# Top-k attention and two gated layers on one core: softmax in place over three score buffers, batch factor on ScalarE, two transposed buffers, two accumulators

## The chip, the cores and the metric

The kernel runs on one core of a Trainium2 chip. Its time is the device time of one execution in microseconds. Beside the plain runs there is one profiled execution, and every row shown below comes from it.

## The reference

Attention over 4 batches, 8 heads, 576 positions of 64 dimensions, in which only the 32 largest scores of a row stay; then a layer 512 to 2048 to 512 with an ELU between, then a gated layer whose two arms are multiplied before a product with two more matrices.

```python
scores = scale * q @ k.T
kth = 32nd largest of each row
scores = where(scores >= kth, scores, -1e9)
attn = exp(scores - max); attn = attn / (sum(attn) + 1e-9)
x = (attn @ v) as [2304 tokens, 512]
h = x @ w_in;  g = where(h > 0, h, exp(min(h, 0)) - 1);  x = g @ w_out
out = ((x @ w1) * (x @ w2)) @ w3 @ w_out2
```

All inputs are float32. The kernel splits a float32 into a high and a low float16 part and multiplies high by high, high by low and low by high, so each product of the layers is three matmuls.

## The kernel before, in words

**Tiling.** 2304 tokens are nine chunks of two tiles of 128 tokens. For each chunk `attention` (L344) goes over four pairs of heads and two tiles, so there are 72 tiles of 128 tokens by 2 heads by 576 keys. `mlp` (L654) then runs the layers of the chunk over its 256 tokens, in units: A (first product and ELU), O (second product), Y (evacuation of the sum and a bound on its norm, from which a scale follows), B (the gated arms), D (last product and output). A chunk's units run one chunk after its attention.

**One attention tile.** TensorE makes the scores of half the keys in `psS` (L383) and ScalarE copies them to a score buffer `s` (L385), twice. VectorE finds the 32 largest of each row and head in place of a sort: four MAX8 (L392) and three MATCH_REPLACE8 (L394) for each head, on a work buffer `wk`. ScalarE computes the masked exponential with a PReLU of huge slope and an Exp (L407, L409) from `s` into a buffer `y`; ScalarE copies `y` to its high half in `pi` (L415), GpSimd subtracts to get the low half (L416), both over the two heads at once. Two transposing DMAs (L419), one for each head, bring `pi` to `pt`. TensorE multiplies `pt` by the values (L431) into the accumulator `psA`; column 64 of each head holds the sum of the weights. VectorE adds 1e-9 to the sums (L440), takes the reciprocal (L441), multiplies the rows of an older batch by the factor `phi` (L443), and multiplies the result by the reciprocal (L444). ScalarE and GpSimd split it (L447, L448), and a DMA transposes it into `x` (L449).

**Buffers.** Two score buffers `s`, two `y`, one `pi`, one `pt`, one `psA`. `psA` and `psN` (256 columns for the norm bound of unit Y, L729 to L735) are columns of one PSUM tile of 512 float32.

**Weights.** The weights come as 64-bit words. Each block is rebuilt to float32 (`load64`, L461: ScalarE, VectorE L477, GpSimd L479), its norm bounded, and scaled and split (`convert`, L499). This runs beside the first chunk's attention. `prep_v` gives each batch of values its scale `sv` and the ratio `phi` to the batch before; `scales` (L543) computes its reciprocal `rho` and constants of the layers.

**What sets the order.** Nothing runs when it is written. Each piece of work is recorded with `op(engine, cost, fn, reads, writes, priority)`. `Program.emit` (L79) plays the costs through a list scheduler: it has one queue for each engine, a latency for each pair of engines (L26), and takes among the ready ops of an engine the one with the lowest rank, where

```python
rank = [o[4] - PAR["cpw"] * cp[i] for i, o in enumerate(self.ops)]
```

The first term is the priority that the op was given, a multiple of STEP plus offsets from `PAR` (L33); the second is its longest path of costs to the end. The order it arrives at is the order in which each engine's instructions are written, and on the chip each engine then runs them in that order and waits where its inputs are late. Semaphores are put in by the tile framework from the tiles that instructions read and write, not from the names used in `op`.

Of the kernel before, what the change touches and what calls it, by code (L numbers as in the profile page):

```python
# [31 lines left out]

PAR = dict(whole=(), cd={'wi': [0, 0], 'wo': [0, 0], 'w34': [8, 0], 'w12': [16, 0]}, pv=115.601, pi=85.231, p34=-12.914, po=349.342, p12=114.078,   # L33
           pis=556.026, pos=-260.711, p12s=-169.557, p34s=-55.646, ci=133.963, co=-112.786, cos=-460.256, c12=-826.201, m34=-813.244, c34=-203.986, 
           m34s=2.143, h34=2, oq=90.567, os=18.83, ok=209.036, ot=363.395, orr=1387.061, opp=-709.446, oa=-95.859, ost=828.567, a0=104.812, a1=106.795, 
           lag0=49.33, lag=24.052, ho=2, h12=0, h12c=7, nr34=2, gm0=1, gm1=1, gm=1, bm=4, cpw=15.144, step=6600.0, pvb=-185.914)

# [112 lines left out]
def kernel(ctx: ExitStack, tc: tile.TileContext, qd, kd, vd, vn, w_in, w_out, w1, w2, w3t, w4, out,  # L150
# [54 lines left out]
    M8 = ring("m8", 4, [128, 2, 32], F32)  # L205
    TY = ring("ty", 4, [128, 16], F32)
# [137 lines left out]
    def attention(c, t0, n):  # L344
# [4 lines left out]
        for pair in range(4):  # L349
# [8 lines left out]
            for t in range(n):  # L358
# [15 lines left out]
                for half in range(2):  # L374
                    cols = slice(half * 288, half * 288 + 288)
                    pqk = pr + (PAR["os"] + .25 * half) * STEP
                    for kk, c0, c1 in ks:

                        def qk(qs=qs, kk=kk, t=t, cols=cols):
                            for i, (L, e) in enumerate(((QH, 0), (QH, 1), (QL, 0))):  # L380
                                for hh in range(2):
                                    hs = slice(64 * hh, 64 * hh + 64)
                                    T.matmul(psS[:, hh, 0:288], lhsT=L[qs][hs, t * 128:t * 128 + 128], rhs=KT[kk][hs, e, cols], start=i == 0, stop=i == 2)  # L383
                        op("PE", 420, qk, [("qh", qs), ("ql", qs), ("k", kk)], ["psS"], pqk)
                        op("ACT", 540, lambda sS=sS, cols=cols, c0=c0, c1=c1: A.activation(sS[c0:c1, :, cols], psS[c0:c1, :, 0:288], AF.Copy, scale=0.125), ["psS"], [sk], pqk)  # L385
# [12 lines left out]
                mx = m8[:, :, 0:1].rearrange("p a b -> p (a b)")  # L398
                tm, dn, ri = [ty[:, 2 * i:2 * i + 2] for i in range(3)]
# [11 lines left out]
                ps, pt = nxt("pi", NPI), nxt("pt", NPT)  # L411
                PIs, pk = PI[ps], ("pi", ps)
                p4 = pr + STEP * PAR["opp"]
                yks = [(*yk, 0), (*yk, 1)]
                op("ACT", 1053, lambda Y=Y, PIs=PIs: A.activation(PIs[:, :, 0:S], Y, AF.Copy), yks, [pk], p4)  # L415
                op("POOL", 2336, lambda Y=Y, PIs=PIs: G.tensor_tensor(PIs[:, :, S:2 * S], Y, PIs[:, :, 0:S], op=OP.subtract),  # L416
                   yks, [pk], p4 + .034 * STEP)
                for hh in range(2):
                    op("SP", 1050, lambda PIs=PIs, pt=pt, hh=hh: Q.dma_start_transpose(out=PT[pt][:, hh], in_=PIs[:, hh]), [pk], [("pt", pt, hh)], p4 - 1e6, lat=1406.0)  # L419
# [3 lines left out]
                p5 = pr + PAR["oa"] * STEP  # L423
                for bb, c0, c1 in segs:
                    vs = Vc[bb, pair]

                    def av(vs=vs, c0=c0, c1=c1, pt=pt):
# [4 lines left out]
                    op("PE", 850, av, [("v", vs), ("vl", vs), ("pt", pt, 0), ("pt", pt, 1)], ["psA"], p5)  # L432

# [4 lines left out]

                def xfin(xf=xf, dn=dn, ri=ri, r1=r1, vb=vb):
# [4 lines left out]
                    V.tensor_tensor(xf.rearrange("p (h d) -> p h d", h=2), psA[:, :, 0:64],  # L444
                                    ri.rearrange("p (h d) -> p h d", d=1).to_broadcast([128, 2, 64]), op=OP.mult)
                op("DVE", 360, xfin, ["psA", *([("phi", vb)] if r1 else [])], [("xf", fs), K("ri")], p5)
                op("ACT", 200, lambda xt=xt, xf=xf: A.activation(xt[:, 0:128], xf, AF.Copy), [("xf", fs)], [("xt", us)], p5)  # L447
# [70 lines left out]
    def prep_v(b, pr):  # L518

        P.tag = "w_v"  # L520
        pieces = []
        for i in range(4):
            if b == 0:
                dst, keys = W12T[:, 2 * i:2 * i + 2].rearrange("p a b -> p (a b)")[:, 0:S], [("w12", 2 * i), ("w12", 2 * i + 1)]
            else:
                rs = nxt("raw", 2)
                dst, keys = raw[rs][:, 0:S], [("raw", rs)]
            dma(dst, vn[b, :, i * S:i * S + S], 128 * S * 4, [], keys, pr)
            pieces.append((dst, keys, S))
        nv, sv, kb = scal(f"nv{b}"), scal(f"sv{b}"), ("nv", b)  # L530
        norm(pieces, nv, kb, pr)
        if b:
            tiny(lambda: V.tensor_tensor(nv, nv, scal(f"nv{b - 1}"), op=OP.max), [("nv", b - 1)], [kb], pr)
        d = sv.bitcast(I32)
        tiny(vts(d, nv.bitcast(I32), 1, 0x3F800000, OP.logical_shift_right, OP.bitwise_and), [kb], [("sv", b)], pr)
        tiny(vts(d, d, -1.0, float((189 + 15) << 23), OP.mult, OP.add), [], [("sv", b)], pr)
        if b:

            r, phi = tmp(16), scal(f"phi{b}")
            tiny(lambda: V.reciprocal(r, scal(f"sv{b - 1}")), [("sv", b - 1)], ["t16"], pr)  # L540
            tiny(lambda: V.tensor_tensor(phi, sv, r, op=OP.mult), [("sv", b), "t16"], [("phi", b)], pr)

    def scales(b, pr):  # L543

        P.tag = "w_v"
        r, phi = scal(f"rho{b}"), scal(f"phi{b}")
        tiny(lambda: V.reciprocal(r, phi), [("phi", b)], [("rho", b)], pr)
        tiny(lambda: V.tensor_tensor(scal(f"c1n{b}"), scal(f"c1n{b - 1}"), r, op=OP.mult), [("rho", b), ("c1n", b - 1)], [("c1n", b)], pr)
# [105 lines left out]
    def mlp(c, t0, n, dprev, pr0, span, hooks=None):  # L654
# [59 lines left out]
        def y_evac(pr):  # L714
# [10 lines left out]
            def gram():  # L725
                for t in range(n):
                    for k in range(4):
                        c = X[:, 0, k, t * 128:t * 128 + 128]
                        T.matmul(psN[:, t * 128:t * 128 + 128], lhsT=c, rhs=c, start=t == 0 and k == 0, stop=k == 3, skip_group_check=True)  # L729
# [3 lines left out]
            op("DVE", 80 + n * 135, lambda: V.tensor_reduce(n1, psN[:, 0:N], axis=AX.X, op=OP.max), ["psN"], [("n1", xs)], pr)  # L733
            op("PE", 240, lambda: T.matmul(psN[:, 0:128], lhsT=n1.to_broadcast([128, 128]), rhs=ident, start=True, stop=True), [("n1", xs), "ident"], ["psN"], pr)
            op("DVE", 200, lambda: V.tensor_reduce(n2, psN[:, 0:128], axis=AX.X, op=OP.max), ["psN"], [("n2", xs)], pr)  # L735
            tiny(vts(n2, n2, 1.02, 1e-30, OP.mult, OP.max), [], [("n2", xs)], pr)
# [174 lines left out]
```

## Time and profile before

| what | value |
|---|---|
| median of 3 runs | 1100.72 us (1099.6 to 1103.41) |
| the profiled execution's own time | 1098.79 us |
| its span | 1097.0 us |
| granted TensorE clock, mean | 0.976 |
| PE, DVE, ACT, POOL busy | 91%, 85%, 74%, 59% of the span |
| PE busy in 40 slices | `4199847699898999999999999999999999999998` |
| DVE busy in 40 slices | `6999899999999989999997999997999999971010` |

Engines: PE is TensorE's matmuls (PEld its weight loads), DVE VectorE, ACT ScalarE, POOL GpSimd, SP the queue of the DMAs. A slice is 27.4 us and a digit is the busy share in tenths. The busy share of PE is of matmuls that overlap, so it tells of back-to-back issue, not of a peak.

### The profile page before, as it was taken

The page shows a single profiled execution, that of the slowest core. Times are in us where ns is not written, and L with a number is a line of the kernel's source. Part 1 is how long each engine was busy: PE and PEld are TensorE (multiplying, and loading weights), DVE is VectorE, ACT ScalarE, POOL GpSimd, SP SyncE. Part 2 cuts the span into 40 slices and gives each one's busy share as a digit, 9 for nine tenths or more (in the row PEclk, how much of TensorE's full clock was granted, in tenths as well). Part 3 has the DMA queues.
Part 4 walks back from the last instruction along what each step waited for, and adds up shares of the span by engine and source line. Part 5 has one row for each costly group of instructions (what it writes and reads, how often), then busy time and mean ns, then how long its engine had stood idle before and what let it go on. Part 6 is the DMA issues. An engine that isn't in the chain of part 4 may idle for free.

```text
span 1097.0 us, 24651 instructions
## 1 busy us (share of the span) xinstructions
PE 996.1 (91%) x9452; PEld 759.1 (69%) x9452; DVE 935.9 (85%) x2024; ACT 807.7 (74%) x1349; POOL 652.0 (59%) x619
## 2 busy tenths in 40 slices
PE   4199847699898999999999999999999999999998
PEld 2144413368777868887886888788778878879875
DVE  6999899999999989999997999997999999971010
ACT  6976789899778966786795688689768857963522
POOL 5479765558536844783685478368537745853711
PEclk9999968799999999999999999999999999999999
DMA  9989973744736586456859545656664652231000
GB/s 364 319 234 339 290 239 129 197 115 109 149 88 177 172 187 147 103 125 163 178 170 224 141 103 113 173 144 166 165 162 97 134 138 71 50 82 37 1 20 20
DMA packets 238678, 165.54 MB, mean 151 GB/s; under 512 B 195808, under 2 KB 208608, under 8 KB 238560
## 3 DMA queue, kind: packets, MB, share of 16 engines
q1 hardware_dynamic: 238560, 163.97, 55.8%
q8 instruction: 74, 1.21, 0.5%
q14 instruction: 44, 0.36, 0.1%
HBM read 95.13 MB, written 21.61 MB: 106 GB/s over the span
## 4 chain that ended last, share of the span: by engine, by line
PE 57%; DVE 23%; ACT 6%; DMA 6%; issue 4%; POOL 3%; SPq 1%; DVEq 0%; POOLq 0%; ACTq 0%
DVE m L392 8%; DVE wk L394 7%; PE psS L383 5%; PE psR L672 4%; PE psR L751 4%; PE psA L431 4%; PE psR L674 4%; PE psR L673 4%; PE psY L709 4%; PE psR L753 4%; PE psR L752 4%; PE psY L710 4%; PE psY L711 4%; DMA pt<-pi 4%; DVE w L477 3%
## 5 line engine op out<-in xcount | busy, mean ns | idle before, releaser
L392 DVE MAX8 m<-wk 128x8 f32<-128x576 f32 x432 | 308.2, 746 | 0.0
L416 POOL TENSOR_TENSOR pi<-y,pi 128x1152 f16<-128x1152 f32 x72 | 172.8, 2400 | 118.5 <-ACT pi L415 108.1
L394 DVE MATCH_REPLACE8 wk<-m,wk 128x576 f32<-128x576 f32 x288 | 211.9, 741 | 0.0
L751 PE MATMUL psR<-x,w 128*128 128x256 f16 x576 | 157.8, 274 | 1.4 <-ACT t L761 1.4
L672 PE MATMUL psR<-x,win 128*128 128x256 f16 x576 | 157.7, 274 | 1.2 <-DMA x<-xt 1.2
L753 PE MATMUL psR<-x,w 128*128 128x256 f16 x576 | 157.4, 273 | 0.0
L752 PE MATMUL psR<-x,w 128*128 128x256 f16 x576 | 157.4, 273 | 0.0
L709 PE MATMUL psY<-g,wout 128*128 128x256 f16 x576 | 157.4, 273 | 0.0
L674 PE MATMUL psR<-x,win 128*128 128x256 f16 x576 | 157.3, 273 | 0.0
L673 PE MATMUL psR<-x,win 128*128 128x256 f16 x576 | 157.3, 273 | 0.0
L710 PE MATMUL psY<-g,wout 128*128 128x256 f16 x576 | 157.0, 273 | 0.3 <-POOL g L696 0.3
L711 PE MATMUL psY<-g,wout 128*128 128x256 f16 x576 | 157.0, 273 | 0.0
L407 ACT ACTIVATE y<-s,m 128x576 f32<-128x576 f32 x144 | 106.4, 772 | 51.1 <-DVE m L392 46.6
L383 PE MATMUL psS<-kt,qh 64*128 64x288 f32 x640 | 91.1, 362 | 35.3 <-ACT s L385 27.1
L385 ACT ACTIVATE s<-psS 128x576 f32<-128x576 f32 (+1 forms) x160 | 103.3, 646 | 20.8 <-PE psS L383 19.6
L409 ACT ACTIVATE y<-y,ty 128x576 f32<-128x576 f32 x144 | 108.6, 774 | 6.8 <-POOL ty L402 6.7
L392 DVE MAX8 m<-s 128x8 f32<-128x576 f32 x144 | 101.9, 744 | 7.6 <-ACT s L385 7.6
L394 DVE MATCH_REPLACE8 wk<-m,s 128x576 f32<-128x576 f32 x144 | 105.9, 741 | 0.0
L383 PEld LDWEIGHTS psS<-kt,qh 64*128 64x128 f32 x640 | 50.9, 195 | 70.8 <-ACT s L385 36.2
L696 POOL TENSOR_TENSOR g<-t,g 128x512 f16<-128x512 f32 x72 | 84.4, 1174 | 22.2 <-ACT g L695 21.7
L431 PEld LDWEIGHTS <-pt 128*128 128x128 f16 (+1 forms) x2240 | 80.5, 103 | 22.0 <-DMA pt<-pi 12.5
L431 PE MATMUL psA<-vv,pt 128*128 128x65 f16 (+3 forms) x2240 | 86.0, 197 | 10.4 <-DMA pt<-pi 10.3
(164 smaller groups left out, 2318.2 us busy)
## 6 DMA issues: line engine op xcount, KB each, us to landing
kt<-kd SPq DMA_DIRECT2D x32, 576.0 KB, 4.2
vv<-vd SPq DMA_DIRECT2D x32, 455.0 KB, 3.9
kd<-kt SPq DMA_DIRECT2D x16, 576.0 KB, 4.1
wout<-w_in SPq DMA_DIRECT2D x16, 512.0 KB, 8.7
w<-w3t SPq DMA_DIRECT2D x16, 512.0 KB, 4.8
w<-w_out SPq DMA_DIRECT2D x16, 512.0 KB, 4.5
vd<-vv SPq DMA_DIRECT2D x16, 455.0 KB, 5.2
w<-w SPq DMA_DIRECT2D x12, 512.0 KB, 7.0
```

The costliest lines, as they stand in the source:

```text
L392: op("DVE", 665, lambda r=r, src=src, m8=m8, hh=hh: V.max(m8[:, hh, 8 * r:8 * r + 8], src), [skey], [mk], p1 + PAR["ot"] * STEP)
L394: op("DVE", 727, lambda r=r, src=src, w=w, m8=m8, hh=hh: V.match_replace(w, m8[:, hh, 8 * r:8 * r + 8], src, -3.0e38), [skey, mk], [k], p1 ...
L431: T.matmul(psA[c0:c1, hh, 0:d], lhsT=PT[pt][:, hh, j % 9, c0:c1], rhs=VV[vs][:, j, hh, 0:d], start=j == 0, stop=j == 13, skip_group_check= ...
L672: T.matmul(o, lhsT=hi(W)[:, cs], rhs=X[:, 0, kd_, 0:N], start=kd_ == 0, stop=False)
L673: T.matmul(o, lhsT=hi(W)[:, cs], rhs=X[:, 1, kd_, 0:N], start=False, stop=False)
L674: T.matmul(o, lhsT=lo(W)[:, cs], rhs=X[:, 0, kd_, 0:N], start=False, stop=kd_ == 3)
L709: T.matmul(o, lhsT=hi(W)[:, cs], rhs=rh, start=ft == 0 and m % 2 == 0, stop=False, skip_group_check=True)
L710: T.matmul(o, lhsT=hi(W)[:, cs], rhs=rl, start=False, stop=False, skip_group_check=True)
L711: T.matmul(o, lhsT=lo(W)[:, cs], rhs=rh, start=False, stop=ft == 15, skip_group_check=True)
L751: T.matmul(o, lhsT=hi(W)[:, cs], rhs=X[:, 0, kd_, 0:N], start=kd_ == 0, stop=False)
L752: T.matmul(o, lhsT=hi(W)[:, cs], rhs=X[:, 1, kd_, 0:N], start=False, stop=False)
L753: T.matmul(o, lhsT=lo(W)[:, cs], rhs=X[:, 0, kd_, 0:N], start=False, stop=kd_ == 3)
```

## The change

- `y` goes: PReLU and Exp write into the score buffer itself, which is held until the high and low halves have been made from it. There are three score buffers in place of two.
- L415 and L416 become one instruction for each head, and each head's transposing DMA depends on its own half.
- There are two `pt` buffers and two accumulators `psA`, in columns 0 to 129 and 130 to 259 of the same PSUM tile; `psN` is 128 columns and sums both tiles of the chunk.
- The sum plus 1e-9 is made by ScalarE, which for the rows of the older batch also multiplies by `rho` (the reciprocal of `phi`), so no factor is left to apply; where a tile holds both kinds of rows there are two such instructions. VectorE is left with the reciprocal, an op of its own, and the multiplication. `rho` is computed in `prep_v`, ahead of `scales`.
- The scheduler's cost for the score matmuls goes from 420 to 500, those of the norm bound and of the split ops follow their new sizes, and all the coefficients in `PAR` that set offsets and the weight of the longest path are other numbers.

```diff
-PAR = dict(..., pv=115.601, pi=85.231, p34=-12.914, po=349.342, p12=114.078, pis=556.026, pos=-260.711, ... cpw=15.144, ...)
+PAR = dict(..., pv=2349.675, pi=182.585, p34=-2331.198, po=92.909, p12=1602.432, pis=1638.166, pos=-1488.916, ... cpw=561.362, ...)
-    NQ, NK, NV, NS, NY, NPI, NPT, NT2, NG = 2, 3, 4, 2, 2, 1, 1, 5, 3
+    NQ, NK, NV, NS, NPI, NPT, NT2, NG = 2, 3, 4, 3, 1, 2, 5, 3
-    YY = ring("y", NY, [128, 2, S], F32)
-    psA, psN = psAT[:, 0:130].rearrange("p (h d) -> p h d", h=2), psAT[:, 130:386]
+    psAs = [psAT[:, 130 * i:130 * i + 130].rearrange("p (h d) -> p h d", h=2) for i in range(2)]
+    psN = psAT[:, 260:388]
-                        op("PE", 420, qk, ...)
+                        op("PE", 500, qk, ...)
-                ys = nxt("y", NY)
-                Y, yk = YY[ys], ("y", ys)
+                Y, yk = sS, sk
-                op("ACT", 1053, lambda Y=Y, PIs=PIs: A.activation(PIs[:, :, 0:S], Y, AF.Copy), yks, [pk], p4)
-                op("POOL", 2336, lambda Y=Y, PIs=PIs: G.tensor_tensor(PIs[:, :, S:2 * S], Y, PIs[:, :, 0:S], op=OP.subtract),
                 for hh in range(2):
+                    pk, hks = ("pi", ps, hh), [(*yk, hh), sk]
+                    op("ACT", 573, ... A.activation(PIs[:, hh, 0:S], Y[:, hh], AF.Copy), hks, [pk], p4 + .5 * hh * STEP)
+                    op("POOL", 1240, ... G.tensor_tensor(PIs[:, hh, S:2 * S], Y[:, hh], PIs[:, hh, 0:S], op=OP.subtract),
+                       hks, [pk], p4 + (.034 + .5 * hh) * STEP)
                     op("SP", 1050, ... Q.dma_start_transpose(out=PT[pt][:, hh], in_=PIs[:, hh]), [pk], [("pt", pt, hh)], p4 - 1e6, lat=1406.0)
-                    V.tensor_scalar(dn, psA[:, :, 64], 1e-9, None, op0=OP.add)
-                    V.reciprocal(ri, dn)
-                    if r1:
-                        V.tensor_scalar(ri[0:r1], ri[0:r1], scal(f"phi{vb}")[0:r1], None, op0=OP.mult)
+                for c0, c1 in ((0, r1), (r1, 128)):
+                    if c0 < c1:
+                        sc_, sk_ = (scal(f"rho{vb}")[c0:c1], [("rho", vb)]) if c0 < r1 else (1.0, [])
+                        op("ACT", 190, ... A.activation(dn[c0:c1], psA[c0:c1, :, 64], AF.Copy, scale=sc_, bias=1e-9), [pak, *sk_], [K("dn")], p5)
+                op("DVE", 70, lambda dn=dn: V.reciprocal(dn, dn), [K("dn")], [K("ri")], p5)
-                        T.matmul(psN[:, t * 128:t * 128 + 128], lhsT=c, rhs=c, start=t == 0 and k == 0, stop=k == 3, ...)
+                        T.matmul(psN, lhsT=c, rhs=c, start=t == 0 and k == 0, stop=t == n - 1 and k == 3, ...)
```

## Rows read from the trace of the kernel before

**Rows 1.** Windows: busy us of each engine (count), clock, DMA share, GB/s.
```profile
0.00:225.00 225.00, 146.66 (x766) 74.80 (x766) 207.59 (x355) 176.21 (x300) 143.87 (x116) 0.91 0.81 261
225.00:300.00 75.00, 70.51 (x731) 56.14 (x730) 72.73 (x171) 68.08 (x116) 50.50 (x48) 1.00 0.53 125
300.00:985.00 685.00, 671.08 (x7044) 541.25 (x7045) 644.03 (x1466) 525.90 (x870) 417.56 (x416) 0.99 0.57 139
985.00:1022.00 37.00, 37.00 (x359) 32.71 (x357) 5.65 (x19) 15.88 (x29) 17.58 (x18) 1.00 0.13 33
1022.00:1097.00 75.00, 70.89 (x560) 54.19 (x557) 5.92 (x15) 21.64 (x37) 22.51 (x22) 1.00 0.04 15
```

**Rows 2.** The line of the first layer's product: durations min/median/max, first and last start.
```profile
L672 PE MATMUL psR<-x,win x576: 270/273/421, 225.7 to 1040.9; 128*128 128x256 f16 x192
```

**Rows 3.** Windows of VectorE's weight rebuilding (L477) alone: DVE busy us (count).
```profile
0.00:225.00 225.00, 85.30 (x71) 0.91 0.81 261
225.00:1097.00 872.00, 0.71 (x1) 0.99 0.50 123
```

**Rows 4.** TensorE's waits, 300 us to the end: total us, times, longest.
```profile
PE psA L431 <- DMA pt<-pi: 8.9, 9, 2.1
PE psS L383 <- ACT s L385: 2.7, 4, 1.0
```

**Rows 5.** Groups of VectorE: shapes, count | busy us, mean ns | idle before.
```profile
L444 DVE TENSOR_TENSOR xf<-psA,ty 128x128 f32<-128x128 f32 x72 | 21.0, 292 | 8.1 <-DVE ty L441 0.5 <-DVE ty L443 0.5
...
L441 DVE RECIPROCAL ty<-ty 128x2 f32<-128x2 f32 x72 | 11.9, 166 | 2.5
L440 DVE TENSOR_SCALAR ty<-psA 128x2 f32<-128x2 f32 x72 | 10.8, 150 | 20.4 <-PE psA L431 12.6 <-PE psA L729 4.9 <-PE psA L734 2.5
...
L443 DVE TENSOR_SCALAR ty<-ty,sc 128x2 f32<-128x2 f32 x8 | 5.7, 712 | 0.3
...
L443 DVE TENSOR_SCALAR ty<-ty,sc 64x2 f32<-64x2 f32 x8 | 4.4, 547 | 0.3
...
L733 DVE TENSOR_REDUCE ac<-psA 128x1 f32<-128x256 f32 x9 | 3.7, 415 | 4.4 <-PE psA L729 4.4
L735 DVE TENSOR_REDUCE ac<-psA 128x1 f32<-128x128 f32 x9 | 2.5, 282 | 4.5 <-PE psA L734 4.5
```

**Rows 6.** Groups of ScalarE and GpSimd, columns as above.
```profile
L416 POOL TENSOR_TENSOR pi<-y,pi 128x1152 f16<-128x1152 f32 x72 | 172.8, 2400 | 118.5 <-ACT pi L415 108.1 <-DMA raw<-vd 4.8 <-DVE m L392 3.8
...
L696 POOL TENSOR_TENSOR g<-t,g 128x512 f16<-128x512 f32 x72 | 84.4, 1174 | 22.2 <-ACT g L695 21.7
L415 ACT ACTIVATE pi<-y 128x1152 f16<-128x1152 f32 x72 | 83.6, 1161 | 12.5 <-DMA pt<-pi 11.6 <-ACT y L409 0.5
...
L770 ACT ACTIVATE t<-psR,sc 128x256 f32<-128x256 f32 x54 | 25.3, 469 | 34.6 <-PE psR L753 32.8 <-issue 1.7
...
L447 ACT ACTIVATE xt<-xf 128x128 f16<-128x128 f32 x72 | 22.2, 309 | 25.6 <-DVE xf L444 24.2 <-DMA vv<-vd 0.9
```

**Rows 7.** Waits of the DMA queue: total us, times, longest.
```profile
SPq L419 <- PE psA L431: 25.9, 12, 4.1
```

**Rows 8.** One tile on ScalarE in order of time: start us, us, what.
```profile
654.34 0.65 ACT L385 ACTIVATE s<-psS 128x576 f32<-128x576 f32 x1
...
677.55 1.43 ACT L407 ACTIVATE y<-s,m 128x576 f32<-128x576 f32 x2
...
679.55 0.64 ACT L385 ACTIVATE s<-psS 128x576 f32<-128x576 f32 x1
...
682.52 0.64 ACT L385 ACTIVATE s<-psS 128x576 f32<-128x576 f32 x1
```

**Rows 9.** The same tile on GpSimd, in order of time.
```profile
682.57 2.38 POOL L416 TENSOR_TENSOR pi<-y,pi 128x1152 f16<-128x1152 f32 x1
```

**Rows 10.** VectorE's end of the attention, in order of time.
```profile
980.43 0.75 DVE L392 MAX8 m<-wk 128x8 f32<-128x576 f32 x1
985.33 0.16 DVE L440 TENSOR_SCALAR ty<-psA 128x2 f32<-128x2 f32 x1 [4.15 <-PE psA L729]
```

More of the change, by code (lines that the diff above doesn't have):

```diff
@@ L31 @@
 FLAT = 2.0 ** -100
[L33 to L36, printed above, removed]
+PAR = dict(whole=(), cd={'wi': [0, 0], 'wo': [0, 0], 'w34': [8, 0], 'w12': [16, 0]}, pv=2349.675, pi=182.585, p34=-2331.198, po=92.909, p12=1602.432,
+           pis=1638.166, pos=-1488.916, p12s=-234.543, p34s=-487.755, ci=1027.823, co=-590.374, cos=-1703.978, c12=-917.975, m34=-1164.921,
+           c34=-818.054, m34s=-330.825, h34=2, oq=-760.206, os=-1061.422, ok=1838.368, ot=1555.123, orr=1125.094, opp=-1061.962, oa=-79.762,
+           ost=35.521, a0=353.379, a1=159.194, lag0=388.249, lag=-220.864, ho=2, h12=0, h12c=7, nr34=2, gm0=1, gm1=1, gm=1, bm=4, cpw=561.362,
+           step=6600.0, pvb=-968.21)
 def conv_modes(n, d, g):
@@ L205 @@
     M8 = ring("m8", 4, [128, 2, 32], F32)
-    TY = ring("ty", 4, [128, 16], F32)
+    TY = ring("ty", 4, [128, 4], F32)
     psS = psum.tile([128, 2, 512], F32, name="psS")
     psAT = psum.tile([128, 512], F32, name="psA")
-    psA, psN = psAT[:, 0:130].rearrange("p (h d) -> p h d", h=2), psAT[:, 130:386]
+    psAs = [psAT[:, 130 * i:130 * i + 130].rearrange("p (h d) -> p h d", h=2) for i in range(2)]
+    psN = psAT[:, 260:388]
     psY = ring("psY", 2, [128, 2, 256], F32, psum)
@@ L383, in qk @@
                                     T.matmul(psS[:, hh, 0:288], lhsT=L[qs][hs, t * 128:t * 128 + 128], rhs=KT[kk][hs, e, cols], start=i == 0, stop=i == 2)
-                        op("PE", 420, qk, [("qh", qs), ("ql", qs), ("k", kk)], ["psS"], pqk)
+                        op("PE", 500, qk, [("qh", qs), ("ql", qs), ("k", kk)], ["psS"], pqk)
                         op("ACT", 540, lambda sS=sS, cols=cols, c0=c0, c1=c1: A.activation(sS[c0:c1, :, cols], psS[c0:c1, :, 0:288], AF.Copy, scale=0.125), ["psS"], [sk], pqk)
@@ L398, in attention @@
                 mx = m8[:, :, 0:1].rearrange("p a b -> p (a b)")
-                tm, dn, ri = [ty[:, 2 * i:2 * i + 2] for i in range(3)]
+                tm, dn = [ty[:, 2 * i:2 * i + 2] for i in range(2)]
                 p2 = pr + PAR["orr"] * STEP
@@ L411, in attention @@
                 ps, pt = nxt("pi", NPI), nxt("pt", NPT)
-                PIs, pk = PI[ps], ("pi", ps)
+                PIs = PI[ps]
                 p4 = pr + STEP * PAR["opp"]
-                yks = [(*yk, 0), (*yk, 1)]
-                op("ACT", 1053, lambda Y=Y, PIs=PIs: A.activation(PIs[:, :, 0:S], Y, AF.Copy), yks, [pk], p4)
-                op("POOL", 2336, lambda Y=Y, PIs=PIs: G.tensor_tensor(PIs[:, :, S:2 * S], Y, PIs[:, :, 0:S], op=OP.subtract),
-                   yks, [pk], p4 + .034 * STEP)
                 for hh in range(2):
+                    pk, hks = ("pi", ps, hh), [(*yk, hh), sk]
+                    op("ACT", 573, lambda Y=Y, PIs=PIs, hh=hh: A.activation(PIs[:, hh, 0:S], Y[:, hh], AF.Copy), hks, [pk], p4 + .5 * hh * STEP)
+                    op("POOL", 1240, lambda Y=Y, PIs=PIs, hh=hh: G.tensor_tensor(PIs[:, hh, S:2 * S], Y[:, hh], PIs[:, hh, 0:S], op=OP.subtract),
+                       hks, [pk], p4 + (.034 + .5 * hh) * STEP)
                     op("SP", 1050, lambda PIs=PIs, pt=pt, hh=hh: Q.dma_start_transpose(out=PT[pt][:, hh], in_=PIs[:, hh]), [pk], [("pt", pt, hh)], p4 - 1e6, lat=1406.0)
@@ L423, in attention, with av @@
                 p5 = pr + PAR["oa"] * STEP
+                pa = nxt("psA", 2)
+                psA, pak = psAs[pa], ("psA", pa)
                 for bb, c0, c1 in segs:
                     vs = Vc[bb, pair]
-                    def av(vs=vs, c0=c0, c1=c1, pt=pt):
+                    def av(vs=vs, c0=c0, c1=c1, pt=pt, psA=psA):
                         for hh in range(2):
@@ L431, in av @@
                                 T.matmul(psA[c0:c1, hh, 0:d], lhsT=PT[pt][:, hh, j % 9, c0:c1], rhs=VV[vs][:, j, hh, 0:d], start=j == 0, stop=j == 13, skip_group_check=True)
-                    op("PE", 850, av, [("v", vs), ("vl", vs), ("pt", pt, 0), ("pt", pt, 1)], ["psA"], p5)
+                    op("PE", 850, av, [("v", vs), ("vl", vs), ("pt", pt, 0), ("pt", pt, 1)], [pak], p5)
                 fs, us = nxt("xf", NX), nxt("xt", 2)
@@ L437, in attention, with xfin @@
                 r1 = min(128, S * vb - tok) if b0 < vb else 0
-                def xfin(xf=xf, dn=dn, ri=ri, r1=r1, vb=vb):
-                    V.tensor_scalar(dn, psA[:, :, 64], 1e-9, None, op0=OP.add)
-                    V.reciprocal(ri, dn)
-                    if r1:
-                        V.tensor_scalar(ri[0:r1], ri[0:r1], scal(f"phi{vb}")[0:r1], None, op0=OP.mult)
+                for c0, c1 in ((0, r1), (r1, 128)):
+                    if c0 < c1:
+                        sc_, sk_ = (scal(f"rho{vb}")[c0:c1], [("rho", vb)]) if c0 < r1 else (1.0, [])
+                        op("ACT", 190, lambda psA=psA, dn=dn, c0=c0, c1=c1, sc_=sc_: A.activation(dn[c0:c1], psA[c0:c1, :, 64], AF.Copy, scale=sc_, bias=1e-9), [pak, *sk_], [K("dn")], p5)
+                op("DVE", 70, lambda dn=dn: V.reciprocal(dn, dn), [K("dn")], [K("ri")], p5)
+                def xfin(xf=xf, dn=dn, psA=psA):
                     V.tensor_tensor(xf.rearrange("p (h d) -> p h d", h=2), psA[:, :, 0:64],
-                                    ri.rearrange("p (h d) -> p h d", d=1).to_broadcast([128, 2, 64]), op=OP.mult)
-                op("DVE", 360, xfin, ["psA", *([("phi", vb)] if r1 else [])], [("xf", fs), K("ri")], p5)
+                                    dn.rearrange("p (h d) -> p h d", d=1).to_broadcast([128, 2, 64]), op=OP.mult)
+                op("DVE", 208, xfin, [pak, K("ri"), K("dn")], [("xf", fs)], p5)
                 op("ACT", 200, lambda xt=xt, xf=xf: A.activation(xt[:, 0:128], xf, AF.Copy), [("xf", fs)], [("xt", us)], p5)
@@ L541, in prep_v @@
             tiny(lambda: V.tensor_tensor(phi, sv, r, op=OP.mult), [("sv", b), "t16"], [("phi", b)], pr)
+            tiny(lambda: V.reciprocal(scal(f"rho{b}"), phi), [("phi", b)], [("rho", b)], pr)
     def scales(b, pr):
@@ L546, in scales @@
         r, phi = scal(f"rho{b}"), scal(f"phi{b}")
-        tiny(lambda: V.reciprocal(r, phi), [("phi", b)], [("rho", b)], pr)
         tiny(lambda: V.tensor_tensor(scal(f"c1n{b}"), scal(f"c1n{b - 1}"), r, op=OP.mult), [("rho", b), ("c1n", b - 1)], [("c1n", b)], pr)
@@ L728, in gram @@
                         c = X[:, 0, k, t * 128:t * 128 + 128]
-                        T.matmul(psN[:, t * 128:t * 128 + 128], lhsT=c, rhs=c, start=t == 0 and k == 0, stop=k == 3, skip_group_check=True)
+                        T.matmul(psN, lhsT=c, rhs=c, start=t == 0 and k == 0, stop=t == n - 1 and k == 3, skip_group_check=True)
             n1, n2, al, co = AC[xs][:, 0:1], AC[xs][:, 1:2], scal(f"al{xs}"), scal(f"co{xs}")
             op("PE", 60 * 4 * n, gram, [("xh", xs, k) for k in range(4)], ["psN"], pr)
-            op("DVE", 80 + n * 135, lambda: V.tensor_reduce(n1, psN[:, 0:N], axis=AX.X, op=OP.max), ["psN"], [("n1", xs)], pr)
-            op("PE", 240, lambda: T.matmul(psN[:, 0:128], lhsT=n1.to_broadcast([128, 128]), rhs=ident, start=True, stop=True), [("n1", xs), "ident"], ["psN"], pr)
-            op("DVE", 200, lambda: V.tensor_reduce(n2, psN[:, 0:128], axis=AX.X, op=OP.max), ["psN"], [("n2", xs)], pr)
+            op("DVE", 200, lambda: V.tensor_reduce(n1, psN, axis=AX.X, op=OP.max), ["psN"], [("n1", xs)], pr)
+            op("PE", 240, lambda: T.matmul(psN, lhsT=n1.to_broadcast([128, 128]), rhs=ident, start=True, stop=True), [("n1", xs), "ident"], ["psN"], pr)
+            op("DVE", 200, lambda: V.tensor_reduce(n2, psN, axis=AX.X, op=OP.max), ["psN"], [("n2", xs)], pr)
             tiny(vts(n2, n2, 1.02, 1e-30, OP.mult, OP.max), [], [("n2", xs)], pr)
```

## The prediction

> **What bounds the kernel now.** I read the windows first, split where the stages change: first layer's start, the steady stretch, the end of attention, the last chunk. TensorE is busy 146.7 of the first 225 us, 70.5 of the next 75, and 671.1 of the 685 us from 300 to 985 [rows 1]. So from 300 us on the kernel issues matmuls nearly back to back, and TensorE is what ends last. VectorE is close behind: 207.6 of 225, 72.7 of 75, 644.0 of 685 [rows 1]. Two engines are near their limit, so what matters is which of them has work waiting at the end. VectorE's last MAX8 ends at 980.43 + 0.75 = 981.2 us [rows 10]. From 985 to 1022 TensorE is busy 37.0 of 37 us [rows 1] on the chunk before the last. It is behind VectorE by about 37 us when the attention is over. From 1022 the last chunk's layers take 75 us, of which 4.1 are idle [rows 1].
>
> Then I asked when the first layer starts: its first matmul is at 225.7 us [rows 2]. By then 71 of 72 instructions by which VectorE rebuilds weights are done, 85.3 us of its 225 [rows 3]. The first layer needs only the blocks of its own matrix. So TensorE's stream begins late, at a point set by VectorE's order of work, and runs without a gap from then on. Last, TensorE's waits after 300 us: 8.9 us for the transposed weights of the softmax and 2.7 us for the evacuation of scores [rows 4]; its idle time there is 13.9 + 0 + 4.1 = 18.0 us [rows 1].
>
> From this follow two rules for the sum. Work taken off VectorE counts only if TensorE gets to start or go on earlier by it. And time on ScalarE and GpSimd counts only where TensorE or VectorE is kept waiting.
>
> **The change part by part.**
>
> *Off VectorE.* L440 goes: 72 x 0.150 = 10.8 us. L443 goes: 5.7 + 4.4 = 10.1 us. L733 reads 128 columns in place of 256, so it costs what L735 costs, 9 x (0.415 - 0.282) = 1.2 us [rows 5]. Together 22.1 us of busy time. The 20.4 us that VectorE idled before L440 [rows 5] pass to the lone reciprocal, which waits for ScalarE: between all of it gone and the same again, and I take no change. On the end of the kernel the 22 us are worth nothing by themselves, since TensorE has its 37 us of backlog to work off. If the steps below take TensorE 29 us forward and VectorE ends 22 us sooner, 30 us of backlog are left, so this cover holds. Behind a waiting reciprocal stand the next MAX8 and MATCH_REPLACE8, that is the next tile's softmax.
>
> *Onto ScalarE.* The sums take 72 instructions, and 8 more where a tile holds rows of two batches (the 64-row form of L443 tells their number), so 80. No instruction of ScalarE on two columns is in the trace. The nearest rows: L447 has 0.309 us at 128 columns and L415 1.161 at 1152, so 0.83 ns a column and 0.204 us at two columns; L770, which reads PSUM, has 0.469 at 256, so 0.258 [rows 6]. I take 0.23, between them: 80 x 0.23 = 18.4 us. Splitting L415 by heads gives 0.682 us each by the same slope, 72 x (2 x 0.682 - 1.161) = 14.6 us. ScalarE has 159 us idle between 300 and 985 [rows 1], which hide the 33 us. In the first 225 us it idles 49 us; the share of nine tiles of 72 there is 4 us, hidden too. Without that cover each tile would pay 0.46 us in its own chain.
>
> *GpSimd.* L416 is 2.400 us at 1152 columns and L696 1.174 at 512, so 1.297 at 576, and 72 x (2 x 1.297 - 2.400) = 14.0 us more, beside 267 us idle from 300 to 985 [rows 1, 6]. Against this, GpSimd waits 108.1 us in all for L415 [rows 6], and the first head's transposing DMA can now go after 0.68 + 1.30 = 1.98 us in place of 3.56 for both. That, and a second `pt` buffer, which takes away the 25.9 us in which the transposing DMAs stood behind L431 [rows 7], bear on the 8.9 us of TensorE. The third score buffer and the exact cost of the score matmuls bear on the 2.7 us. Of these 11.6 us I take 9. The ends are a loss of 9 (waits doubled) and the whole 18.0 us of idle time.
>
> *Softmax in place.* What changes is how long a score buffer is held. One tile: first written at 654.34, read last by L407 at 677.55 + 1.43 = 678.98; the next evacuation into that buffer starts 0.6 us later, at 679.55, and ends at 683.16 [rows 8]. So now the evacuation starts the moment a buffer is free. Held until the low half is made, to 682.57 + 2.38 = 684.95 [rows 9], the buffer is taken for 30.6 us in place of 24.6. With a third buffer the next user comes one tile later. A tile's period is (981.2 - 225) / 63 = 12.0 us (63 of the 72 tiles come after the first layer's start), so the slack grows by 12.0 - 6.0 = 6 us. I cost the longer hold at nothing; its cover is these 6 us, and a tile whose low half is made later than that pays the excess on VectorE.
>
> *The order.* All offsets are new, and the longest path weighs 561 times its length in place of 15, against a time term that is unchanged. This is the largest unknown. What the trace does say: weights cannot come further ahead of the first layer, for nearly all are ahead of it already [rows 3]. So the move that is open is towards an earlier start. TensorE idles 78.3 + 4.5 = 82.8 us before 300 [rows 1], the outer end of a gain. VectorE, which sets that start, idles 17.4 + 2.3 = 19.7 us there [rows 1]; closing those gaps needs no work moved behind the first layer. I take 20. The other end is a loss of the same 20, gaps twice as wide.
>
> *The sum.* The profiled execution took 1098.79 us, 1.8 around a span of 1097.0. 1098.8 - 9 - 20 = 1069.8, so 1070. It is 1.9 us under the median of the three runs, which is less than they differ among themselves, and I add nothing for it.
>
> **The rivals.**
>
> *The start stays (1090).* The new order moves nothing before 300 us, and only TensorE's waits go: 1098.8 - 9 = 1090, between 1081 and 1099. For it speaks that TensorE's matmuls after 225.7 us are the same in number; against it the 19.7 us of gaps and the order of the weights. Chance 0.18.
>
> *Much earlier (1050).* Weights that the first layer does not need move behind it and TensorE loses its backlog. The limit is then VectorE's end plus the last chunk: 1098.8 - 22 - 37 = 1040. Half of the way from the forecast to it is about 1055, so this case is 1040 to 1055. For it speak the 85.3 us of rebuilding ahead of the first matmul [rows 3]; against it that the second and third layers need their blocks soon after. Chance 0.12.
>
> *Slower: the two accumulators share one tile (1118).* The scheduler counts them as two and may order the next tile's L431 right behind the last. The trace shows what the chip does with columns that are apart but in one tile: L440, which reads columns of `psA`, idled 4.9 us for L729, which writes columns of `psN` [rows 5], once for 4.15 us [rows 10]. So L431 would stand on TensorE, and the whole matmul queue behind it, until the sum, reciprocal and multiplication before it are done: 0.23 + 0.166 + 0.292 = 0.7 us, a hop between engines and up to one instruction of 1.16 us ahead of it on ScalarE [rows 5, 6], about 2 us. At 24 of the 72 tiles that is 48 us: 1098.8 - 29 + 48 = 1118. It decides from 15 tiles on (30 us, the gain of the forecast). Against it: one VectorE feeds the tiles 12 us apart, so few pairs should come that close. Chance 0.20.
>
> The Trainium skill speaks for this rival: "PSUM — Partial Sum Buffer", section "PSUM bank collisions raise a hardware error", says that two engines must not touch one bank in the same partitions at once, whichever columns, and wants semaphores by bank. By that rule a second accumulator in the same 512-float tile buys TensorE no overlap; by the scheduler's names it buys all of it. The 4.9 us at L440 are on the rule's side.
>
> **How the numbers follow.** The forecast has 0.50, with 1055 to 1085 as its own range. A run within 0.3% of the time before (1097 to 1104) cannot be told from no change. The forecast and the much earlier case are faster by more than that (0.62); of the rival with an unchanged start 0.08 is faster, 0.08 the same and 0.02 slower; of the slower one 0.01 is the same and 0.19 slower. Together 0.70, 0.09 and 0.21. The range goes from 1042, just inside VectorE's limit, to 1112, which holds a part of the slower case.
>
> **What would show it.** The first L672 about 20 us earlier, near 206 us, or the step on the order is wrong. TensorE's idle time after 300 us near 9 us, with L431's wait for `pt` almost gone. VectorE's busy time near 914 us, ScalarE's near 841, GpSimd's near 666. VectorE's wait for scores no larger than before. TensorE without a gap when the attention ends, or the 22 us of VectorE would count after all. The prediction is wrong if TensorE shows waits at L431 for VectorE's multiplication or ScalarE's sum of more than some 30 us, or if the first layer starts later than 226 us.

## The result, and the profile after

The changed kernel takes 1072.24 us (median, 1070.34 to 1073.18) against 1101.92 us of the kernel before in the same runs: a ratio of 0.973 (95% interval 0.9706 to 0.9754). The profiled execution took 1072.09 us, its span is 1069.9 us.

The first thing to read is the first layer's first matmul, the line that answers to [rows 2]: durations min/median/max, then first and last start.

```profile
L677 PE MATMUL psR<-x,win x576: 270/273/421, 200.5 to 1014.1; 128*128 128x256 f16 x192
```

It starts at 200.5 us in place of 225.7, that is 25.2 us earlier, and the span is 27.1 us shorter. So I split both traces at that matmul. Windows of the kernel before, then of the changed one; the columns are those of [rows 1].

```profile
0.00:225.70 225.70, 147.36 (x772) 75.23 (x772) 208.29 (x357) 176.91 (x301) 144.07 (x117) 0.91 0.81 260
225.70:1097.00 871.30, 848.78 (x8682) 683.87 (x8680) 727.64 (x1668) 630.81 (x1049) 507.96 (x503) 0.99 0.50 123
```

```profile
0.00:200.50 200.50, 141.22 (x766) 73.63 (x767) 184.78 (x337) 167.52 (x299) 138.50 (x117) 0.92 0.91 278
200.50:945.00 744.50, 728.88 (x7626) 587.02 (x7625) 697.38 (x1562) 610.69 (x1122) 484.31 (x530) 0.99 0.59 142
945.00:1069.90 124.90, 121.12 (x1063) 95.59 (x1061) 13.58 (x39) 45.73 (x82) 43.95 (x45) 1.00 0.11 29
```

After the first matmul the old kernel needs 871.3 us and the new one 744.5 + 124.9 = 869.4. TensorE's work there is the same, 848.8 against 850.0 us, and its idle time 22.5 against 19.4. Nearly the whole gain lies before the first layer. VectorE is what fills that stretch in both: 208.3 of 225.7 us, then 184.8 of 200.5. Its rebuilding of weights alone, by windows of that line:

```profile
0.00:225.70 225.70, 85.30 (x71) 0.91 0.81 260
...
```

```profile
0.00:200.50 200.50, 69.42 (x64) 0.92 0.91 278
```

Seven instructions moved behind the first layer and the rest became shorter; that is 15.9 of the 23.5 us of VectorE that went. The other 7.6 are further instructions with two inputs that became shorter and small pieces left for later. Its top-k there is the same, 9.8 and 10.0 tiles.

What TensorE waits for from 300 us to the end, the answer to [rows 4], and then VectorE's waits for scores, from the list of all waits:

```profile
PE psS L384 <- ACT s L386: 3.2, 3, 1.5
PE psA L433 <- DVE xf L449: 0.5, 1, 0.5
```

```profile
DVE m L393 <- ACT s L386: 22.2, 11, 8.0
```

The wait for `pt` is gone from TensorE after 300 us. VectorE waits longer for scores than before (22.2 us against 7.6), and it costs nothing: from 945 us on, when the last top-k is over (945.2), TensorE is still busy 121.1 of 124.9 us.

The pieces that changed, in the columns of [rows 5]:

```profile
L417 POOL TENSOR_TENSOR pi<-s,pi 128x576 f16<-128x576 f32 x144 | 186.3, 1305 | 100.2 <-ACT pi L416 82.6 <-issue 10.5 <-DMA pt<-pi 3.5
...
L416 ACT ACTIVATE pi<-s 128x576 f16<-128x576 f32 x144 | 94.6, 679 | 20.3 <-DMA pt<-pi 19.9
...
L444 ACT ACTIVATE ty<-psA 128x2 f32<-128x2 f32 x56 | 9.5, 170 | 13.8 <-PE psA L433 12.2 <-DVE ac L738 1.2 <-DVE xf L449 0.3
...
L738 DVE TENSOR_REDUCE ac<-psA 128x1 f32<-128x128 f32 x9 | 2.6, 287 | 10.9 <-PE psA L734 8.3 <-PE psA L433 2.6
```

### The profile page after: what moved, and what is told of

It reads as the page before. It is cut to its first block, busy times and chain, and to the rows that moved or that the text cites. A ratio compares the mean times of both kernels' runs of the same rounds, so it can differ in the third digit from the quotient of the medians.

```text
span 1069.9 us, 24966 instructions
## 1 busy us (share of the span) xinstructions
PE 991.2 (93%) x9452; PEld 756.2 (71%) x9452; DVE 895.7 (84%) x1936; ACT 823.9 (77%) x1501; POOL 666.8 (62%) x691
## 4 chain that ended last, share of the span: by engine, by line
PE 70%; ACT 9%; DVE 8%; DMA 7%; issue 4%; POOL 2%; SPq 0%; POOLq 0%; DVEq 0%; ACTq 0%
PE psS L384 7%; PE psR L756 6%; PE psR L758 6%; PE psR L757 6%; PE psR L677 5%; PE psA L433 5%; PE psR L679 5%; PE psR L678 5%; PE psY L714 5%; PE psY L716 5%; PE psY L715 5%; DMA pt<-pi 4%; PE psR L791 3%; PE psR L793 3%; PE psR L792 3%
## 5 line engine op out<-in xcount | busy, mean ns | idle before, releaser
L417 POOL TENSOR_TENSOR pi<-s,pi 128x576 f16<-128x576 f32 x144 | 186.3, 1305 | 100.2 <-ACT pi L416 82.6
L386 ACT ACTIVATE s<-psS 128x576 f32<-128x576 f32 (+1 forms) x160 | 103.8, 649 | 35.7 <-PE psS L384 29.4
L393 DVE MAX8 m<-s 128x8 f32<-128x576 f32 x144 | 102.3, 744 | 22.2 <-ACT s L386 22.2
L384 PE MATMUL psS<-kt,qh 64*128 64x288 f32 x640 | 90.1, 360 | 30.1 <-ACT s L386 23.5
L407 ACT ACTIVATE s<-s,m 128x576 f32<-128x576 f32 x144 | 107.6, 774 | 10.6 <-DVE m L393 10.4
L416 ACT ACTIVATE pi<-s 128x576 f16<-128x576 f32 x144 | 94.6, 679 | 20.3 <-DMA pt<-pi 19.9
L409 ACT ACTIVATE s<-s,ty 128x576 f32<-128x576 f32 x144 | 106.3, 771 | 3.1 <-POOL ty L403 3.0
L699 POOL TENSOR_TENSOR t<-t,t 128x512 f32<-128x512 f32 x72 | 93.0, 1292 | 3.5 <-ACT t L698 0.7
```

The source lines that it names most:

```text
L393: op("DVE", 665, lambda r=r, src=src, m8=m8, hh=hh: V.max(m8[:, hh, 8 * r:8 * r + 8], src), [skey], [mk], p1 + PAR["ot"] * STEP)
```

## The experiments

Twelve kernels were run, each timed against the kernel before. "Start" is the first start of the first layer's matmul, "stream" the span from there to the end, both in the profiled execution. Run 6 is the changed kernel up to its start and run 7 nearly so; their 197.6 and 198.9 us beside 200.5 show how far a start differs by itself.

| kernel | time, us | ratio to before (95%) | start | stream | TensorE idle in the stream |
|---|---|---|---|---|---|
| before | 1101.9 | | 225.7 | 871.3 | 22.5 |
| changed | 1072.2 | 0.973 (0.971 to 0.975) | 200.5 | 869.4 | 19.4 |
| 1 new coefficients, old parts | 1141.7 | 1.037 (1.033 to 1.041) | 237.0 | 903.2 | 35.7 |
| 2 new parts, old coefficients | 1119.8 | 1.017 (1.013 to 1.022) | 235.4 | 887.6 | 45.0 |
| 3 changed, path weight 500 | 1079.7 | 0.980 (0.977 to 0.983) | 211.6 | 866.5 | 19.1 |
| 4 before, path weight 13.5 | 1099.1 | 0.999 (0.997 to 1.000) | 229.5 | 867.7 | 24.9 |
| 5 VectorE work added early | 1095.6 | 0.995 (0.994 to 0.997) | 225.4 | 868.3 | 17.3 |
| 6 VectorE work added late | 1078.5 | 0.980 (0.976 to 0.983) | 197.6 | 878.3 | 25.7 |
| 7 sums on VectorE again | 1072.4 | 0.974 (0.971 to 0.977) | 198.9 | 873.7 | 20.9 |
| 8 one `pt` | 1081.1 | 0.982 (0.979 to 0.985) | 211.5 | 867.7 | 16.7 |
| 9 one accumulator | 1068.0 | 0.970 (0.967 to 0.973) | 210.6 | 854.5 | 12.9 |
| 10 halves of both heads joined | 1130.8 | 1.028 (1.024 to 1.032) | 240.0 | 888.7 | 27.7 |
| 11 two score buffers | 1122.5 | 1.020 (1.017 to 1.023) | 232.4 | 887.0 | 29.2 |
| 12 remainders on TensorE | 1075.4 | 0.976 (0.973 to 0.980) | 204.3 | 868.7 | 17.5 |

**First question: the coefficients or the parts?** My first theory was that the new coefficients bring the start forward by themselves; the rival, that the new parts do.

*1, the kernel before with the new coefficients.*
```diff
-PAR = dict(..., cpw=15.144, ...)        # all the old numbers
+PAR = dict(..., cpw=561.362, ...)       # all the new numbers
-                        op("PE", 420, qk, ...)
+                        op("PE", 500, qk, ...)
```


> The kernel before with only the coefficients of the scheduler and the cost of the score matmuls taken from the change. Theory 1 (the coefficients bring the first layer's start forward, and the rest of the stream is as long as it was): first layer's matmul near 203 us, total 1073 to 1083. Rival (the parts - three score buffers, halves by head, two transposed buffers, the sum on ScalarE - free VectorE and the buffers, and the coefficients only fit them): first layer near 225 us, total 1092 to 1110, since the old buffers then stand in the new order's way.

*2, the changed kernel with the old coefficients.*
```diff
-PAR = dict(..., cpw=561.362, ...)
+PAR = dict(..., cpw=15.144, ...)
-                        op("PE", 500, qk, ...)
+                        op("PE", 420, qk, ...)
```


> The changed kernel with the old coefficients and the old cost of the score matmuls, so only the parts are new. Theory 1: the first layer starts within 5 us of 225.7, total 1090 to 1100. Rival (the parts do it): first layer near 203 us, total 1070 to 1080.

Both expectations fail. The coefficients alone cost 41 us, the parts alone 19, and together they gain 30. Neither starts early. In run 1 the first layer waits for its own weights: the line that makes their low halves starts at 208.5 us, in the changed kernel at 132.9 (durations, first and last start; run 1, then the changed kernel).

```profile
L514 PE MATMUL psY<-win,si x24: 592/592/1220, 208.5 to 236.4; 128*128 128x512 f32 x24
```

```profile
L518 PE MATMUL psY<-win,si x24: 592/697/1222, 132.9 to 167.4; 128*128 128x512 f32 x24
```

VectorE has run 12.1 tiles of top-k by the first matmul there, where the first chunk needs eight and the changed kernel has done ten. In run 2 the weights are in time (their low halves begin at 146.4 us) and the eighth tile is late: its top-k is over at 193.2 us, in the changed kernel at 169.9. VectorE idles 29.9 us ahead of the first matmul there, against 15.7; what puts the tile so late no run took apart.

The start is the smaller part of both losses. Against the kernel before, run 1 loses 11.3 us at the start and 31.9 behind it, run 2 9.7 and 16.3. In run 1 TensorE soon has little to run again; here is a window of 25 us behind its start, in the columns of [rows 1]:

```profile
287.00:312.00 25.00, 12.89 (x71) 6.93 (x72) 22.97 (x39) 22.77 (x41) 18.82 (x15) 0.67 0.80 217
```

In the stream of run 2 the tiles wait on ScalarE's sums and TensorE on scores. These are VectorE's and TensorE's longest waits (VectorE's of the whole span, of which 0.6 us lie before the start; TensorE's from 235 us on):

```profile
DVE ty L445 <- ACT ty L443: 45.7, 29, 10.7
```

```profile
PE psS L383 <- ACT s L385: 36.4, 14, 9.0
```

*3 and 4, the weight of the longest path moved by a tenth, in the changed kernel and in the one before.*
```diff
-... cpw=561.362, ...
+... cpw=500.0, ...
```
```diff
-... cpw=15.144, ...
+... cpw=13.5, ...
```


> The changed kernel with the weight of the longest path at 500 in place of 561.362, everything else as it is: how far any small shift of the order moves the time. Theory 1 says that the time goes with the first layer's start: total = that start + 869 us within 6 us, whatever it is. If the coefficients are tuned to a point, the start moves by 5 to 20 us and the total by the same; if not, total within 3 us of 1072.

> The kernel before with the weight of the longest path at 13.5 in place of 15.144: the same question for the old parts. Theory 1: total = first layer's start + 871 us within 6 us. Rival (the old parts make the steady stretch uneven, so any order of them has more idle time after the start): the sum is more than 880 us after the start.

These are the scale for the rest: a small shift of the order moves the changed kernel by 7.5 us, with a start 11.1 us later (211.6) and a stream 2.9 shorter, and the kernel before by less than 2, with a start 3.8 later and a stream 3.6 shorter. Totals are start plus stream within the 6 us that was set: 211.6 + 866.5 and 229.5 + 867.7. One shift of one coefficient is a small sample, but a part undone with the order planned anew says nothing below some 8 us.

**Second question: is it VectorE's time before the first layer that counts?** Here the order of the changed kernel was kept as it is.

*5 and 6, 80 unused instructions on VectorE, early or late.*
```diff
+        dve = [k for k, (t, i) in enumerate(order) if self.ops[i][0] == "DVE" and 20000.0 <= t < 160000.0]   # run 6: 330000 to 800000
+        pick = {dve[j * len(dve) // 80] for j in range(80)}
-        for _, i in order:
+        for k, (_, i) in enumerate(order):
             self.ops[i][2]()
+            if k in pick:
+                self.extra()    # nc.vector.tensor_scalar(dummy, ident, 1.0, None, op0=OP.mult)
```


> The changed kernel in its own order, with 80 extra small VectorE instructions (128x128, some 0.23 us each, 18 us in all) spread between its own over the stretch in which the first chunk's attention and the weights are prepared; their result is used nowhere. Theory 1b (VectorE's instructions up to the eighth tile of the first chunk set the first layer's start, and the rest follows at fixed length): start 16 to 20 us later, total 1086 to 1094. Rival (the start is set by the chain of ScalarE, GpSimd and DMAs behind the tiles): start at most 8 us later, total under 1081.

> The same 80 extra VectorE instructions, spread over the middle of the program (planned times 330 to 800 us). Theory 1b: TensorE has work waiting there, so 18 us more on VectorE are hidden: total 1071 to 1076. Rival (VectorE is what ends the attention and so the kernel, and the change helps by taking work off it): total 1084 to 1092.

Windows of run 5, then of run 6, each split at its first layer:

```profile
0.00:225.40 225.40, 148.75 (x766) 77.86 (x767) 209.80 (x416) 168.27 (x299) 136.06 (x117) 0.88 0.82 248
225.40:1093.70 868.30, 850.99 (x8687) 683.01 (x8685) 710.10 (x1601) 656.50 (x1204) 529.05 (x575) 0.99 0.52 126
```

```profile
0.00:197.60 197.60, 136.14 (x767) 70.73 (x768) 186.53 (x335) 165.98 (x297) 136.85 (x116) 0.96 0.92 282
197.60:1075.90 878.30, 852.56 (x8687) 683.06 (x8685) 739.64 (x1682) 657.16 (x1205) 530.26 (x576) 0.99 0.51 125
```

Early, VectorE's time before the first layer grows from 184.8 to 209.8, by 25.0 us. The start moves by 24.9 and the total by 23.4, with the stream as it was (868.3). The instructions were longer than I had priced them: the 80 take 40.0 us by themselves, while VectorE's rebuilds there became 8.0 us shorter (below). So the rise exceeds the expected 14 to 22 us, and the start moves one for one with VectorE's time. GpSimd waited for these instructions too, 14.1 us in five waits, but it idles 89 us of that stretch. Late, VectorE is busy 30.4 us longer in all (926.2 against 895.7) and the total rises by 6.3, more than the 4 us I allowed; the stream of the profiled execution is 8.9 longer, behind a start that was 2.9 earlier. Together these two settle the question: before the first layer a microsecond of VectorE counts nearly whole, behind it two to three tenths.

*7, the sums on VectorE, at the same places.*
```diff
-... A.activation(dn[c0:c1], psA[c0:c1, :, 64], AF.Copy, scale=sc_, bias=1e-9)
+... V.tensor_scalar(dn[c0:c1], psA[c0:c1, :, 64], 1e-9, sc_, op0=OP.add, op1=OP.mult)
```


> The changed kernel in its own order, with the 80 instructions that make the sums (plus 1e-9, times the batch factor) on VectorE at the same places in place of ScalarE. Theory 1b: VectorE gets some 13 us more, nearly all of it after the first layer's start: total 1072 to 1076. Rival (the relief of VectorE is what the change gains by): total 1082 to 1090.

1072.36 us against 1072.24, with 11.5 us more on VectorE (907.2 in all). The relief of VectorE by this part, in this order, buys nothing.

**Third question: which parts does the new order need?** One part undone at a time, the coefficients kept, the order planned anew.

*8, one transposed buffer; 9, one accumulator; 11, two score buffers.*
```diff
-NQ, NK, NV, NS, NPI, NPT, NT2, NG = 2, 3, 4, 3, 1, 2, 5, 3
+NQ, NK, NV, NS, NPI, NPT, NT2, NG = 2, 3, 4, 3, 1, 1, 5, 3      # run 8
+NQ, NK, NV, NS, NPI, NPT, NT2, NG = 2, 3, 4, 2, 1, 2, 5, 3      # run 11
-                pa = nxt("psA", 2)
+                pa = nxt("psA", 1)                              # run 9
```


> The changed kernel with one transposed buffer in place of two, the order planned anew for it. If the second buffer is what lets the new coefficients put off the multiplication with the values while weights and top-k go on (in the changed kernel the median tile has 26 us from its last MAX8 to its division, before 18): the first layer starts 10 to 35 us later, total 1085 to 1120. If the buffer only removes a small wait: total 1070 to 1080.

> The changed kernel with one accumulator in place of two, the order planned anew. In the changed kernel no tile's multiplication with the values begins before the one before it has been divided, so the second accumulator is never used at the same time as the first. If so it carries nothing: total 1070 to 1080, the width being what a small shift of the order made (8 us). If it does carry the order: over 1085.

> The changed kernel with two score buffers in place of three, softmax still in place, the order planned anew. In the changed kernel the scores of the tile after next begin before a tile's low half is made for 67 of 70 tiles, so with two buffers VectorE has to wait for scores of nearly each tile: VectorE's waits for scores over 100 us, total 1150 to 1300. Rival (a later evacuation is enough): total under 1100.

With one `pt` the start is 11 us later, within what I set for a buffer that carries the order, and the total 9, below it. That is near what a shift of the order does, so the second buffer's worth stays open between nothing and some 9 us. One accumulator is no slower: 1068.0 us, the fastest of all that ran, though its interval (0.967 to 0.973) touches that of the change. Its start is 10 us later; its gain over the change is in the stream (854.5 against 869.4, with TensorE 8.5 us less busy and 6.5 less idle) and may be the order's luck. So between two orders the start alone does not tell the time.

The premise of its expectation is wrong. In the changed kernel eight tiles' products with the values do begin before the tile ahead of them is divided, so the second accumulator is used; in the kernel before and in run 9 none does. In one such pair the tile ahead had its product by 174.25 us; these are the next tile's product and then the division of the tile ahead (start, us, what, idle time before it and what ended it):

```profile
176.64 0.58 PE L433 MATMUL psA<-vv,pt 128*128 128x65 f16 x14
177.80 0.60 PE L433 MATMUL psA<-vv,pt 128*128 128x65 f16 x14 [0.58 <-DMA pt<-pi]
178.50 0.29 DVE L449 TENSOR_TENSOR xf<-psA,ty 128x128 f32<-128x128 f32 x1 [0.78 <-PE psA L433]
```

The division waits until the product into the other columns is done, and in each of the eight pairs it starts behind that product. That run 9 loses nothing shows that the overlap is not needed.

With two score buffers the time is 50 us above the change, but for another reason than I gave. VectorE's longest wait in run 11:

```profile
DVE m L393 <- ACT s L386: 57.4, 23, 10.3
```

That is 57 us, not over 100; and the low halves of the first layer's weights come late (first at 191.7 us), as in run 1.

*10, the halves of both heads made together.*
```diff
-                for hh in range(2):
-                    op("ACT", 573, ... PIs[:, hh, 0:S], Y[:, hh] ...)
-                    op("POOL", 1240, ... PIs[:, hh, S:2 * S] ...)
+                op("ACT", 1053, ... PIs[:, :, 0:S], Y ...)
+                op("POOL", 2336, ... PIs[:, :, S:2 * S] ...)
```


> The changed kernel with the high and low halves of both heads made by one ScalarE and one GpSimd instruction again, the order planned anew. If the halves by head only shorten a chain that is not waited for: total 1068 to 1080. If the transposing DMAs of the first chunk are what the eighth tile waits for: first layer 10 us or more later and total over 1082.

59 us more than the change, and the start at 240.0 us. The chain behind the tiles is not what makes it late. From the end of the eighth tile's top-k to its landing in `x` it is 31.8 us (190.7 to 222.5), in the change 30.0 (169.9 to 199.9); the top-k itself comes 20.8 us later. What comes last is again the first layer's weights:

```profile
L518 PE MATMUL psY<-win,si x24: 592/684/1200, 204.1 to 232.3; 128*128 128x512 f32 x24
```

By the first matmul VectorE has done 12.8 tiles of top-k, in run 11 12.9, in run 1 12.1. In the changed kernel and in runs 3, 5 to 9 and 12 it is 9.8 to 10.8 tiles, and none of them is above 1096 us. The three are slow in the same way: more top-k stands ahead of the first layer's weights. The low halves need an identity matrix times the weights' scale (`si`), which VectorE makes at 202.0 us in run 10, 191.4 in run 11 and 206.0 in run 1, after 9.1, 8.8 and 9.1 tiles of top-k; in the changed kernel it is made at 132.6, after 5.5. So most of what moved ahead is the first chunk's own top-k, with about one tile of the second; the rest of the 12 tiles ran while TensorE made the low halves. What the joined op, the second score buffer and the old parts have in common is a longer path through the attention, by which the scheduler ranks; that this is why they change places is argued from the code, not shown by a run.

*12, the low halves of the last product's weights on TensorE.*
```diff
-... cd={'wi': [0, 0], 'wo': [0, 0], 'w34': [8, 0], 'w12': [16, 0]} ...
+... cd={'wi': [0, 0], 'wo': [0, 0], 'w34': [0, 0], 'w12': [16, 0]} ...
```


> The changed kernel with the low halves of the eight blocks of the product of the last two matrices made on TensorE and ScalarE, as for the first two layers, and not on VectorE; the order planned anew. If VectorE's time before the first layer sets the total: the 6.0 us that it spends there on these blocks go, the start is 3 to 10 us earlier and the total 1060 to 1070. If the order's own scatter is larger than that: 1066 to 1082 with a start to match. Rival (TensorE, which makes these halves then, is late): first layer later than 205 us and total over 1078.

1075.4 us with the start at 204.3. VectorE's 6.0 us on these blocks went, but the new order did 0.8 tiles more of top-k ahead of the first layer, which costs as much. It falls in the scatter of the order, as the middle case had it.

## Why the prediction was right, point by point

*What bounds.* TensorE, back to back from the first layer on, and a start that VectorE's order sets: shown by run 5 for the start and by run 6 for what follows, up to the two to three tenths that late work on VectorE cost there.

*The order, 20 us.* Measured 25.2. It was sized by the 19.7 us of gaps on VectorE, and this is not where it came from: VectorE's idle time before the first layer went from 17.4 to 15.7 us only. It was work that went: seven rebuilds put behind the first layer, the others shorter (1.085 us each against 1.201), and 7.6 us of other instructions, shorter or left for later. The number was near by luck, the reason for it was not right; the rows that carried the better reason were [rows 3], which I used for the direction alone.

*TensorE's waits, 9 us.* From 300 us to the end its idle time fell from 18.0 to 7.5 us (762.4 of 769.9 busy), so 10.5, and the wait for `pt` there is gone. But measured from the start of the stream it fell by 3.1: some idle time now lies between 200 and 300 us. This term was counted in a window that the earlier start moved. The sum 9 + 20 = 29 against 26.7 in the profiled executions hides that one term was low by 5 and the other high by 6. That they cancel is luck.

*Two terms as if they could be added.* The parts and the order were priced apart. Runs 1 and 2 show that they can't: +41 and +19 apart, -30 together. No step of the prediction said so.

*VectorE's relief counts nothing.* Right for a relief of this size, by run 7 and by the 121.1 of 124.9 us at the end; the 30 us of run 6 were not free. Its size was wrong: busy time fell by 40.2 us, not 22.1. The removed instructions account for what was worked out; most of the rest is the shorter rebuilds and other instructions with two inputs (last section).

*ScalarE and GpSimd.* The sums cost 9.5 + 2.0 + 2.0 + 1.3 = 14.8 us for a forecast of 18.4, the split copies 94.6 - 83.6 = 11.0 for 14.6, GpSimd's split 186.3 - 172.8 = 13.5 for 14.0; its total of 666.8 is the forecast 666. ScalarE's, 823.9, is 17 under. All hidden.

*Softmax in place, nothing.* The median tile's scores stand some 5 us before VectorE takes them, as in the kernel before: the cover held. That VectorE would wait no longer for scores was wrong (22.2 against 7.6 us), without effect.

*The rivals.* The unchanged start is out. The much earlier start did not come: only seven rebuilds moved. The shared tile did not bite: TensorE waited once, 0.5 us, for a division. The mechanism is there, but it falls on the other side. In eight pairs the order put the next product ahead of the division, so VectorE waited: 1.8 us in two waits of the division, and 2.6 us where L738, which reads `psN`, waits for L433, which writes `psA`. These waits are for semaphores that the program holds, in the prediction's example too: they show how it orders the instructions, and what the chip would do without them no run shows. Of the 2330 matmuls into this tile none overlaps in time with any of the 170 instructions that read it. That agrees with what the Trainium skill says under "PSUM bank collisions raise a hardware error" on its page "PSUM — Partial Sum Buffer", which wants such accesses kept apart by semaphores.

## What to carry to other kernels

Where one engine runs back to back to the end, ask what sets its first instruction, and price an edit by whether it stands before or behind that point: here 25 us of VectorE before it cost 23, and 30 us behind it cost 6. Look at the stream behind that point as well: two orders can differ there by more than in the start, as run 1 (31.9 us) and run 9 (14.9 us) do. Where a scheduler writes the order, its coefficients and the program's parts are one edit; undoing either alone measures a third kernel. Before reading a part's worth from such a run, move a coefficient a little and see how far the time goes by itself.

## What the runs showed of the hardware that was not expected

VectorE's rebuild of weights has two inputs from SBUF. In the changed kernel 19 of its 72 instructions ran with no tensor-tensor operation of GpSimd beside them and took 0.68 us each; the 53 others took 1.26 on average. MAX8 takes 0.745 us with or without GpSimd (465 and 111 counted). The line shows the spread as min/median/max:

```profile
L482 DVE SCALAR_TENSOR_TENSOR w<-w x44: 661/1086/1805, 12.8 to 232.6; 128x512 int32<-128x512 int32 x44
```

The unused instructions of runs 5 and 6, of one input, float32 to float16, took 0.21 to 0.23 us alone and 0.67 and 0.53 beside GpSimd, so that the 80 took 40.0 and 34.4 us and not 18. In run 5 VectorE's time grew by less, 25.0 us, since rebuilds became shorter at the same time (61.5 us before the first layer, 69.4 in the changed kernel). The Trainium skill, "GPSIMD Engine Reference", section "Specifications", says that GpSimd shares its SBUF interfaces with VectorE for instructions with two SBUF inputs or in a two-port mode. The rebuilds' numbers agree, and MAX8, which has one input, fits; the unused instructions would agree if they ran in such a mode, which no row shows. The scheduler reckons with it: the rebuilds are marked `lk`, and `emit` (L122), when it plays the costs, holds such an op back until GpSimd's instruction is nearly over. So an order that puts GpSimd's instructions elsewhere can make VectorE's rebuilds shorter. That the change gained part of its 15.9 us this way is what the durations suggest; no run took it apart.
